# Moving some VectorE products of an S4-convolution and MLP kernel to GpSimd, with a new written-out order

## The chip, the cores and the metric

One core of a Trainium2 chip runs the kernel. A core has five engines with a queue each, called here as the profile calls them: PE (TensorE, matmuls), ACT (ScalarE), DVE (VectorE), POOL (GpSimd) and SP (SyncE, which issues most DMAs). A queue is worked off in order; between queues there are semaphores. The metric is the device time of one execution in microseconds, lower is better. Three runs of the kernel before took 517.82, 519.9 and 520.2 us, median 519.9.

## The reference

The input is `u` of 2048 tokens by 512 channels, in float32. With `xn = layernorm(u)` the output is `u + s * silu(b)`.

`s` is a long convolution per channel (S4): from complex parameters A, B and C of 512 channels by 128 states and a step `dt = exp(log_dt)` a kernel of 2048 taps is made,

```python
logdA = dt * A                       # 512 x 128, complex
P = exp(logdA[:, :, None] * l)       # l = 0 .. 2047
K = einsum("dn,dnl,dn->dl", C, P, dt * B).real
s = irfft(rfft(pad(xn)) * rfft(pad(K)))[:2048] + xn * Dskip
```

`b` is a mixer: `h = gelu(layernorm(xn) @ w1)`, whose four channel groups are shifted by +1, −1, +2 and −2 tokens, then `x1 = xn + shifted(h) @ w2`, then `b = x1 + gelu(layernorm(x1) @ w3) @ w4` with 1376 hidden channels.

## The kernel before, in words

The kernel is written as a plan. Python code calls `V`, `A`, `T`, `Q` (DVE, ACT, PE, SP) and `E` (either ACT or DVE) in the order of the mathematics; each call becomes an operation of the plan with a number, the engines that may do it (`alts`), a cost and the operations it depends on. Nothing is issued then. At the end `Plan.issue` walks through `ORDER`, a text of 1583 numbers, and issues the operations in that order. So every engine's queue is its part of that text. A mark behind a number chooses the engine where there is a choice: a for ACT, v for DVE, no mark for the first of `alts`. The profile therefore puts every operation on one line, L309, and tells them apart by the names of their tiles.

The work falls into these parts:

- Parameters (`params`, operations 36 to 77). Some thirty small steps on tiles of 128 x 512 make, for every channel and state, the logarithm of the decay (`pn[:, 0]`), the phase per step, the start phase and the amplitude. They need A, B, C and `log_dt`; scratch is the tile `tm`. PE transposes the four results, and four copies of 128 x 512 bring them into `par`.
- Token mixing (`token_mixing`): layer norm of X, transposes, `w1` (three of eight pairs of token groups in float32, five in split float16), gelu to `hT`, then `w2` with the shifts. On the way X's first transform is made (`u_stage1`, tile `ue`, stored to `scr_Ud`). The weights w3 and w4 are read once for a scale (`weight_squares`, tile `wst`) and once to be split (`prep`).
- Tables (`tables`): the kernel K in 16 chunks of 32 channels, in four blocks of four. A block makes exponentials per row (`EB`, `mag`, on ACT) and phases (`pab`). A chunk then makes phases in 32-bit integers in a tile `wv` (three DVE instructions), takes cosine and sine on ACT (three instructions of 128 x 2080), and multiplies by magnitudes on DVE (`factors` and `sums`): `eg` from two parts of `EB`, `wv` by `eg` (128 x 2048), the lower half from `mag` and the upper (128 x 2048), `up` from two parts of `mag`, and two products of `wv` by `up`. Then 256 records of matmul on `wv` give the taps (`pc<-wv`), and a first transform (`kev`, `k1e`) goes to memory.
- MLP (`mlp`, eight groups of 256 tokens): per step 24 matmuls by w3 (`pb`), gelu (`g32`), a split of the result in two float16 halves (`ghl`, one scaling on ACT or DVE, one difference on DVE), and 12 matmuls by w4 (`pa`).
- Products (`products`, 16): spectra of X and K by matmuls, a complex product on DVE (`pr`, `kh`), the inverse (`z1e`) to memory. Eight of them are interleaved with chunks 8 to 15 and the MLP, eight come after.
- End: `inverse` and `finish`: the last transform, times silu, plus the input, stored.

Tiles lie at addresses written out by hand. The ring `egr` has two places, used in turn by `eg` and `up` (and `rem` of a block); so an `eg` can be written when the last one has been read, and the same for `up`. The waves' tiles (`wv`) take turns in two buffers, `phA` and `phB`; `pn` and `tm` of the parameters lie in `phA`, the float32 w1 in `phB`. The matmul `warm` on the identity (operation 2, 40 matmuls) fills PE at the start; operation 1 is a square root on ACT of no further use.

Of the kernel before, what the change touches and what calls it, by code (L numbers as in the profile page):

```python
# [14 lines left out]
ALU = mybir.AluOpType  # L15
# [4 lines left out]
P = 128  # L20
# [6 lines left out]
MAGIC = 12582912.0  # L27
# [11 lines left out]
CQ = 32  # L39
# [71 lines left out]
3 17 78 0 16 42 20 19 36 38 4 31 14 39 44 40 70 15 41 21 43 45 22 8 103 105 1 7 46 106 104 107 5 71a 503 6 47 108 13 2  # L111
109 110 88 111 504 112 89 505 24 48 50 90 114a 79 91 80 506 81 92 113a 115a 93 23 51 94 82 95 83 49 118a 84 85 52 96a
100a 86 87a 508 101 97a 98 509 102a 99a 166 162 160 119 164 167 163 116 9 121 165 120a 117a 18 161 37 168 169 72 10
143 144 170 171 53 172 26 73a 25 54 122 123 511 173 55 124 174 125 175v 178v 140 126 127 177v 11 199v 179a 141 196v
128 215 200 59 146 145 149a 213 32 147a 28 142 27 129 219 56 188 339 180 176v 197 217 60 182v 183 218 270 266 184a 158
130 150 268 131 216 269 185 271 181a 186 191 267 272 214 220 273 132 221 30 274 133 340 148 34 61 189 222 275 152 223
276 277 57 64 224 225 134 62 187 29 192a 193 194a 195 226 58 76 227 345 136v 63 230v 65 231v 516 66 68 190 208 67 202
203 513 211a 212 209v 210 198 229v 69 137 201 138v 74 77a 341 514 515 244 247a 248 235v 75v 245a 228v 507 205 206 207
232v 512 246 510 261 236 237 278 233 234 517 346 249v 139 241 242 135 204 279 518 519 238 239 522 262a 12 263 264a 297
252v 343 243 280 155 240 265 255 256 156 536 537 520 282v 521 253 250 151 251 288v 298v 258 254 300a 538 525 259 299  # L120
# [12 lines left out]
390 641 642 628 669 721a 727 722 708 709 723 485a 717 738 733 745 654 739 670 746 486 671 643a 653 656 675 728a 734a
735 724 729 730 672 731 644 673 674 740 657 658 747 645 752 753 741a 646a 676 787 742 820 660 788 736 659 759a 647a
789 760a 754 795 648 678 767 768 748a 791 774 677 797 661 662 663a 790 737 798 743 744 438 440 460 749 750 751 755a
775 761 762 763a 792 793 664 799 680 665 666a 756 667a 461 796 458 679 757 794 681 682 758 769 800 781 764a 801 765
776 770a 683a 777a 802 854 684 685 771 803 772 782 453 451 773 834 835 766 1092 1093 1085 1086 778 806 779 804 668 809
836 805 807 459 1094 686a 687a 1087 783a 454 808 780 688 784 837 838 1099 1100 785 1095a 822 810 811 843 1088a 840
1096 812 813 1089 1114 1106a 868 814a 815 1107a 1115 786 839 816 817a 818a 1090 1091 819 1108 1116 869 841 870 842 441
823 1109 1097 1101 1102a 1103 824a 825 826 1110a 856 1111v 827 1098 828 829 1121 871 845 1104 1105 872 873 830 844  # L140
831a 1128 439 1112 1117a 1113 1118 832a 452 846 487 847 848a 874 1122 902 849 903 488 1129 904 1119 1123 850 1134
1130a 1131 1124a 1125 833 855 851a 852a 905 875 857 908 890 858a 876 1135 1136 1120 859 1126 1127 877 860 906 853 1148
878 888 1149 1141 907 861 944 862 863 864 866a 865a 1142 1143 867 889 879 911 880 881 909 1150 1132 936 910 1163 937
1144v 1170 938 1137a 1138 882a 883 939 941 942 884 489 1133 940 1145 946 1164 1171 885a 886a 891 913 947 943 949 950
892a 1139 893 948 1140 922 1151a 894 490 895 1152 1146 1147 887 1153 1155a 1156a 924 896 897 1159a 1157 898 1154 1158
912 951 1160a 1165 899a 914 1166a 915 900a 1161 945 1177 1167 983 984 985 952 1168 916a 917 1169 1172 1162 1183 1173v
958 1174 953 918 1175 954 1176 919a 920a 955 956 989 1178 925 1184 901 923 1179a 926a 927 957 1185 1186a 1190 928 1191
1180 1187 986 1204a 929 1181 930 921 931 1192 1197 932 988 933a 960 959 987 969 971 1182 934a 1198 992 961 935 962
1188 990 963a 1189 970 1199 964 1017 1018 1193a 965 1200a 966a 967a 968 1201 1219 1194 1208a 972 1005 1195 1209a 1019
973a 991 1205a 1212 1213 1206 974 994 1210 1211 975 976 1196 1207 1202 1003 1020 1214 1203 1022 977 978 979 1021 980a  # L150
981a 982 1023 1220 1221 993 1026 995 1222a 1024 1004 996 1232 997a 998 1051 999 1000a 1052 1226 1001a 1006 1215a 1025
1039 1053 1233 1227 1007a 1216 1008 1239 1240 1054 1055 1217 1009 1010 1011 1012 1013 1014a 1015a 1028 1027 1060 1223
1056 1234 1218 1029 1030 1031v 1037 1032 1224 1241 1228v 1033 1002 1034a 1057 1058 1016 1038 1246 1229 1035a 1040 1261
1041a 1042 1059 1036 1043 1044 1539 1071 1484 1045 1046 1253a 1247 1225 1230 1248 1062 1047 1073 1538 1049a 1048a 1050
1061 471 1231 1536 473 1268 472 474 1063 491 1064 492 1269 1065a 1066 1067 1371 1072 1262 1242a 1235v 1068a 1069a 1385
1236 1074 1237 1254v 1075a 1070 1255 1263 1243 1256 1076 1372 1077 1238 1257v 493 1078 1244 1245 1373 1249a 1250 1387
# [1128 lines left out]
```

## Time and profile before

| | |
|---|---|
| Runs | 517.82, 519.9, 520.2 us |
| The profiled execution | 516.23 us, span from first to last instruction 514.4 us |
| Granted TensorE clock | 0.996 |
| Busy: PE, DVE, ACT, POOL | 489.2, 452.4, 404.4, 0.7 us |
| ACT table loads | 57, 73.1 us together |
| Memory traffic | 90.07 MB, 175 GB/s on the mean |

A row of the timeline has its start in us from the span's start, the time it took, the engine, the operation, the tile written and the tiles read, shapes, and in brackets how long the engine stood still before it and what ended that. A row of the groups has the count, the busy time and mean length of one in ns, and the idle time before. A row of a stage has the busy time of PE, PEld (weight loads), DVE, ACT and POOL, with the number of instructions in brackets, then the granted clock, the DMA engines' busy share and GB/s. A matmul in float32 appears as two records. A busy PE is not always PE at its peak, since the ends of matmuls are modelled.

### The profile page before, as it was taken

The numbers are of one execution on the slowest core, as the hardware profiler recorded it, in microseconds if no ns is written. First come the engines' busy times: TensorE is split into PE (matmuls) and PEld (weight loads), VectorE is DVE, ScalarE is ACT, GpSimd is POOL, SyncE is SP. The second block draws the span as 40 slices with busy tenths as digits, with TensorE's granted clock in tenths as the row PEclk, the third lists the DMA queues.
The fourth block names the chain that finished last, engine by engine and source line by source line (L and its number), as shares of the span: only waits on it lengthen the run. The fifth ranks groups of instructions, "written<-read, shape, count | busy, mean of one in ns | idle before, by whom it ended". The sixth has DMA issues, their size and how long they took to land.

```text
span 514.4 us, 14347 instructions
## 1 busy us (share of the span) xinstructions
PE 489.2 (95%) x6209; PEld 313.8 (61%) x6209; DVE 452.4 (88%) x634; ACT 404.4 (79%) x596; POOL 0.7 (0%) x6
## 2 busy tenths in 40 slices
PE   3899899999999999999999989999999999999993
PEld 3766566664555867667566645657565565576451
DVE  5999999999999999999999989999985578756466
ACT  3999999979998599999999999997865356256320
POOL 0000000000000000000000000000000000000000
PEclk9999999999999999999999999999999999999998
DMA  8957999757362650443635646185689998887987
GB/s 227 250 143 246 274 264 267 203 183 164 42 154 59 150 103 2 66 80 42 145 76 133 145 100 149 64 177 164 137 213 249 243 301 253 245 272 226 331 255 206
DMA packets 149393, 90.07 MB, mean 175 GB/s; under 512 B 97681, under 2 KB 135825, under 8 KB 148945
## 3 DMA queue, kind: packets, MB, share of 16 engines
q1 hardware_dynamic: 144800, 84.68, 65.0%
q10 hardware_dynamic: 4528, 4.46, 3.0%
q8 instruction: 49, 0.80, 0.7%
q14 instruction: 16, 0.12, 0.1%
HBM read 52.95 MB, written 29.36 MB: 160 GB/s over the span
## 4 chain that ended last, share of the span: by engine, by line
PE 65%; DVE 16%; ACT 10%; DMA 4%; issue 3%; ACTq 0%; SPq 0%; DVEq 0%
PE pb L309 25%; PE pa L309 22%; PE pc L309 13%; DVE wv L309 5%; PE pd L309 5%; DVE X L309 2%; ACT ue L309 2%; ACT L309 2%; DMA scr_Ud<-ue 2%; ACT mag L309 1%; DMA X<-in_A_u_dram 1%; ACT wv L309 1%; DVE pr L309 1%; DMA x1T<-x1h 1%; DVE eg L309 1%
## 5 line engine op out<-in xcount | busy, mean ns | idle before, releaser
L309 PE MATMUL pb<-x1T,w3h 128*128 128x256 f16 (+1 forms) x1056 | 124.8, 273 | 0.1
L309 PE MATMUL pa<-w4h,ghl 128*128 128x512 f16 (+1 forms) x528 | 122.1, 380 | 0.0
L309 PEld LDWEIGHTS <-w3h 128*128 128x128 f16 (+1 forms) x1056 | 102.0, 100 | 26.3 <-issue 10.7
L309 PEld LDWEIGHTS <-ghl 128*128 128x128 f16 (+1 forms) x528 | 49.1, 98 | 62.4 <-issue 10.2
L309 ACT ACT_TABLE_LOAD x57 | 73.1, 1283 | 4.8 <-issue 3.1
L309 ACT ACTIVATE wv<-wv 128x2080 f32<-128x2080 int32 x32 | 62.9, 1964 | 1.1 <-DVE wv L309 0.9
L309 ACT ACTIVATE g<-pb,wsc 128x512 f32<-128x512 f32 (+1 forms) x48 | 30.6, 649 | 11.5 <-PE pb L309 11.3
L309 DVE TENSOR_TENSOR wv<-wv,eg 128x2048 f32<-128x2048 f32 x16 | 36.6, 2286 | 2.2 <-ACT wv L309 2.0
L309 DVE SCALAR_TENSOR_TENSOR ghl<-g,wsc,ghl 128x512 f16<-128x512 f32 (+1 forms) x48 | 33.2, 701 | 5.9 <-ACT ghl L309 5.8
L309 DVE TENSOR_TENSOR wv<-mag,wv 128x2048 f32<-128x2048 f32 x16 | 36.5, 2284 | 0.0
L309 DVE TENSOR_TENSOR pr<-pd,kh 128x1024 f32<-128x1024 f32 x16 | 19.6, 1224 | 18.5 <-ACT kh L309 13.7
L309 PEld LDWEIGHTS pc<-wv 128*32 128x32 f32 x2048 | 29.9, 109 | 7.9 <-issue 5.1
L309 PE MATMUL pc<-wv 128*32 128x64 f32 x2048 | 32.8, 220 | 1.7 <-issue 1.7
L309 ACT ACTIVATE mag<-par 128x128 f32<-128x128 f32 x132 | 32.9, 462 | 0.0
L309 ACT ACTIVATE wv<-wv,halfpi 128x2080 f32<-128x2080 f32 x16 | 32.8, 2051 | 0.1
L309 ACT ACTIVATE ghl<-g,wsc 128x512 f16<-128x512 f32 (+1 forms) x38 | 25.4, 678 | 6.6 <-PE pa L309 4.5
L309 PE MATMUL pb<-xT,w1h 128*128 128x256 f16 x240 | 27.8, 273 | 0.4 <-DMA xT<-x2h 0.3
L309 PEld LDWEIGHTS <-w1h 128*128 128x128 f16 x240 | 23.1, 98 | 7.5 <-issue 5.0
L309 PE MATMUL pb<-w,hT 128*128 128x512 f32 x58 | 26.8, 599 | 0.0
L309 PE MATMUL pa<-w,hT 128*128 128x512 f32 x58 | 26.5, 598 | 0.0
L309 PE MATMUL pb<-xT,w 128*128 128x256 f32 x96 | 22.6, 384 | 0.7 <-ACT hT L309 0.7
L309 DVE TENSOR_TENSOR wv<-par,ev 128x1056 int32<-128x1056 f32 x16 | 20.1, 1254 | 1.5 <-PE pc L309 1.5
(156 smaller groups left out, 810.6 us busy)
## 6 DMA issues: line engine op xcount, KB each, us to landing
wst<-in_B_w_dram SPq DMA_DIRECT2D x20, 512.0 KB, 4.6
scr_Ud<-ue SPq DMA_DIRECT2D x16, 512.0 KB, 4.7
uin<-scr_Ud SPq DMA_DIRECT2D x16, 512.0 KB, 4.7
scr_Kfa<-k1e SPq DMA_DIRECT2D x8, 512.0 KB, 5.4
cst<-c_gp SPq DMA_DIRECT2D x16, 256.0 KB, 4.8
kin<-scr_Kfa SPq DMA_DIRECT2D x8, 512.0 KB, 4.7
scr_Kfb<-k1e SPq DMA_DIRECT2D x8, 512.0 KB, 5.8
scr_Zda<-z1e SPq DMA_DIRECT2D x8, 512.0 KB, 3.2
```

The lines of the kernel that those rows point to most:

```text
L309: ins = [getattr(self.engines[op.eng], name)(*args, **kw).ins for name, args, kw in op.calls]
```

## The change

A helper `Spare` is added, called `G` in the kernel: its operations may run on DVE or on POOL, and the plan counts POOL at twice DVE's cost. `G` takes the place of `V` in `factors` (the product `eg`), in `sums` (the product `up`) and in 22 steps of `params`. For such an operation the mark a now means POOL. The two halves of w1 in float32 move from `phB` to the places of blocks 8 and 9 of the ring for `hT`. The copies into `par` write in the order of memory (`n p r`) instead of in strides. The constants in the plan stay. The text `ORDER` is another one throughout: the order on each engine, the engine where there is a choice, and the order of DMA issues on SP and ACT.

```diff
 class Plan:
     def __init__(self, nc):
-        self.engines = {"PE": nc.tensor, "ACT": nc.scalar, "DVE": nc.vector, "SP": nc.sync}
+        self.engines = {
+            "PE": nc.tensor, "ACT": nc.scalar, "DVE": nc.vector, "SP": nc.sync, "POOL": nc.gpsimd,
+        }
...
-            op.eng = {"a": "ACT", "v": "DVE"}.get(word[-1]) or list(op.alts)[0]
+            op.eng = {"a": list(op.alts)[-1] if "POOL" in op.alts else "ACT", "v": "DVE"}.get(word[-1]) or list(op.alts)[0]
...
+class Spare:
...
+    def __getattr__(self, name):
+        def call(*args, **kw):
+            cost = dve_cost(name, args)
+            call = (name, args, kw)
+            self.plan.add(
+                {"DVE": (cost, call), "POOL": (2 * cost, call)}, args[:1], [a for a in args[1:] if is_ap(a)]
+            )
+
+        return call
...
-        load_w(w1, w1s, Ring(phB, K4, 2), Q)
+        load_w(w1, w1s, Ring(sblocks + 8 * K4, K4, 2), Q)
...
-        V.tensor_mul(pn[:, 0], raw["Ar"], dtb)
+        G.tensor_mul(pn[:, 0], raw["Ar"], dtb)
...
-        V.tensor_mul(ta, raw["Bi"], raw["Cr"])
-        V.tensor_add(wi, wi, ta)
+        G.tensor_mul(ta, raw["Bi"], raw["Cr"])
+        G.tensor_add(wi, wi, ta)
...
-            E.copy(par[:, k].rearrange("n (p r) -> n r p", r=4), pt.rearrange("n (r p) -> n r p", r=4))
+            E.copy(par[:, k].rearrange("n (p r) -> n p r", r=4), pt.rearrange("n (r p) -> n p r", r=4))
...
-        outer(V.tensor_mul, eg, EB[:, sl, R_EGA : R_EGA + 4], EB[:, sl, R_EGB : R_EGB + 8])
+        outer(G.tensor_mul, eg, EB[:, sl, R_EGA : R_EGA + 4], EB[:, sl, R_EGB : R_EGB + 8])
...
-        V.tensor_mul(up, mag[:, :, low], mag[:, :, 32:33].to_broadcast([P, CQ, 32]))
+        G.tensor_mul(up, mag[:, :, low], mag[:, :, 32:33].to_broadcast([P, CQ, 32]))
```

The two orders begin like this (the first line of each; parameter steps on POOL such as 44a and 45a follow in the second):

```diff
-3 17 78 0 16 42 20 19 36 38 4 31 14 39 44 40 70 15 41 21 43 45 22 8 103 105 1 7 46 106 104 107 5 71a 503 6 47 108 13 2
+0 16 17 3 4 20 36 78 18 15 37v 7 42v 14 41v 8 43v 88 89 72 90 5 6 79 91 80 44a 73a 511 81 82 83 92 19 38 84 85 93 94
```

More of the change, by code (lines that the diff above doesn't have):

```diff
@@ L116 @@
[L116 to L120, printed above, removed]
@@ new lines @@
+228v 182v 341 343 57a 64a 272 504 133 157 148 505 270 190 175a 179v 268 149a 150 342 183 180 184v 269 347 181a 266
+232v 345 267 271 344 506 177v 61a 273 62a 63a 65a 66a 274 349 275 67a 187 191 276 155 156 277 202 192v 231v 68a 205
+206 194a 278 195 208 196v 513 279 280 197 233 199v 200 229v 136v 193 198 201 203 350 355 235v 236 211v 209v 212 244
+514 515 210 138v 348 353 58a 76 137 69 74 204 247a 245a 237 139 135 346 248 31 230v 234 207 508 75v 507 509 525a 282v
+510 517 238 252v 518 77a 246 239 288v 261 253 249v 241 242 250 354 351 240 255 256 264a 262v 297 265 356 361 281v 512
@@ new lines @@
+327 564 404 393 383 384 405 567 552 581 580 535 553a 566 411 568 406 569 336 333 334 582a 585a 407 394 604 408 388 329
+418 419a 403 385 395a 583 596 597 598 425 570a 599 601 602 330 151 571 584 554a 605 420 555 421 424 426 412 572 606
+396 442 607 608 443a 429 600 603 413 573a 586 609 414 427 587 428 445 415 448 435 416 430 574a 422a 610 611 332 417
+618a 409 410 401 446a 444 465 615a 449 450 431 423 462 612 613 335 588 589 629 436 432 433 434 495a 499a 437 590a 630
+468 500v 631 466a 467 501 496a 497 575 591 463a 464 614 632 634 455 633 447 616 635a 469 481 592 593a 502 710a 470 456
@@ new lines @@
+769 752 749 753 754 796 664 665 737 743 744 750 751 666a 791 763a 667a 800 790 770a 781 440 439 792 441 451 452 793
+794 801 774 775 668 680 681 682 802 803 755v 756 757 854 776 764v 758 765 782 453 458 771 809a 772 683v 684 685 834
+805 835 836 777a 778 806a 804 807 686a 687a 837 839 808 838 766 840a 1092 773 783v 1093 810 779 780 811 459 1085 473
+1086 843a 812 813 784 821 785 1087 841 874a 814a 815 816 1099 868 1106a 1088a 1089 786 1094 688 869 870 817a 842 822
+818a 823 845 856 824a 1100 1101 825 826 827 1090 1091 871 1095a 873 872 828 1121 1114 819 1115 829 830 831a 844 877a
@@ new lines @@
+1102v 1103 1096 1122 832v 1110a 833 1107v 1108 1109 846 847 848a 1111v 1112 849 454 487 1097 875 876 1116 474 850 1098
+1117a 488 489 851a 852a 1123 1104 1105 1124a 857 858a 902 903 904 905 855 1128 1129 1113 878 859 1118 908a 1134 1135
+853 907 1141 1142 906 860 861 862 863 864 922 879 911a 1119 866a 1136 1125 888 865v 880 881 1120 1126 1143 882a 909
+910 883 884 867 1127 946 890 936 885a 937 940 886a 490 1130v 1131 1132 913 941 471 912 1155a 1137a 1144a 1145 891 938
+939 892a 1133 889 947 1163 1164 942 893 1148 948 958a 1149 1138 894 895 1156a 896 897 1157 1139 1140 887 944 943 949
@@ new lines @@
+1159a 898 899v 1165 950 951 1146 914 915 945 900a 916a 969 917 1147 1150 1151v 918 1170 1177 1152 1160v 919v 920v 983
+984 1153 1154 1161 1171 952 954 953 955a 1158 1172 924 925 926a 1178 1166v 1167 1173a 985 1168 1169 956 957 901 923
+927 928 929 930 1162 1183 1190 1184 986 988 931 960 959 932 987 933a 1179v 1180 1191 934a 971 961 1192 962 963a 1185
+1174 989a 990 1175 1176 1204a 1017 935 1197 964 1181 965 1198 921 966a 1018 1019 991 970 1186v 1187 967a 968 972 1193v
+1194 1208v 1020 1182 1212 1199 1213 973a 974 1188 992a 1189 1195 1022 994 1021 1003 975 976 1200a 977 472 978 979 981a
@@ new lines @@
+1201 1023a 993 1219 980a 982 1209a 1210 1024 1057a 1005 995 996 1196 997a 998 1202 1205a 999 1206 1051 1214 1215a
+1000a 1001a 1052 1037 1053 1220 1006 1007a 1226 1227 1004 1025 1207 1221 1008 1054 1026a 1203 1216 1217 1218 1056 1039
+1211 1009 1010 1011 1012 1013 1232 1028 1027 1014a 1029 1060a 1030 1002 1015a 1055 1016 1038 1239 1031v 1032 1228v
+1537 1033 1240 1034a 1035a 1229 1040 1036 1058 1222v 1041a 1233 1223 1234 1073 1042 1059 1043 1224 1225 1241 1230 1044
+1045 1046 1047 1049a 1061 1261 1048a 1050 1071 1062 1063 1064 1413 1400 491 492 1065v 1066 1262 1246 493 1371 1072
@@ new lines @@
+1486 1067 1247 1068a 1069a 1235v 1236 1253v 1254a 1231 1488 1070 1074 1538 1237 1372 1238 1075a 1242v 1243 1244 1373
+1255 1076 1256 1248 1249a 1250 1245 1268 1257a 1258a 1251 1077 1079 1386 1078 1080 1387 1259 1081 1083v 1260 1263
+1264a 1082a 1385 494 1275 1374 1376 1252 1375a 1536 1265 1266 1399 1377 1378 1401 1379 1276 1269 1380 1381 1383v 1270
+1271v 1272 1382a 1084 1415 1281 1539 1388 1389a 1390 1267 1277a 1391 1428 1282 1392 1273 1384 1393 1394 1483 1395 1283
+1397a 1493 1441 1274 1278 1396v 1402 1403a 1398 1414 1404 1405 1427 1406 1288 1289 1290 1279 1407 1408 1409 1455 1484
@@ new lines @@
+1310 1410v 1284v 1416 1429 1443 1411a 1418 1295 1296 1285 1280 1286 1442 1302a 1303v 1417a 1419 1420 1421 1422 1457
+1291a 1423 1424v 1311 1304 1305 1430 1425v 1432 1287 1292 1431a 1293 1433 1434 1294 1435 1436 1437 1439v 1412 1471
+1297 1456 1298a 1317 1299 1438a 1306a 1307a 1444 1445a 1446 1440 1308 1447 1300 1318 1448 1312 1324 1496 1449 1450
+1309 1451 1313v 1301 1314 1452a 1458 1507 1453v 1460 1325 1337 1315 1494 1338 1319 1470 1320a 1321 1426 1454 1469
+1459a 1461 1462 1463 1464 1465 1467v 1540 1330 1466a 1472 1473a 1492 1499 1474 1475 1476 1541 1477 1495 1543 1316 1331
@@ new lines @@
+1332 1322 1326a 1542 1468 1478 1479 1344 1481a 1480v 1482 1500 1497 1518 1510 1501 1345 1485 1562 1498 1502 1339 1556
+1323 1327 1333a 1328 1340a 1346 1329 1490 1351 1352 1565 1334 1335 1336 1347v 1503 1508 1521 1353 1511 1527 1489 1512
+1487 1509 1505 1365 1348 1513 1544 1358 1359 1516 1571 1506 1522 1519 1341 1547 1553 1530 1523 1342 1343 1354v 1349
+1350 1515 1355 1366 1360 1361a 1362 1356 1357 1367v 1504 1517 1368 1363 1364 1369 1520 1524 1525 1528 1577 1370 1491
+1531 1529 1545 1532 1548 1514 1546 1554 1533 1549 1526 1555 1534 1550 1535 1557 1563 1558 1566 1551 1564 1552 1559
@@ L172 @@
+1560 1567 1572 1568 1573 1561 1569 1570 1574 1576 1575 1 1578 1579 1580 1582 1581
 """
@@ L385, in __getattr__, with __init__ @@
         return call
+class Spare:
+    def __init__(self, plan):
+        self.plan = plan
+    def __getattr__(self, name):
[6 more added lines that the diff above has]
+        return call
 class Either:
@@ L633, in params @@
         pn = phtile([P, 4, 4, NM], "pn")
-        V.tensor_mul(pn[:, 0], raw["Ar"], dtb)
+        G.tensor_mul(pn[:, 0], raw["Ar"], dtb)
         V.scalar_tensor_tensor(pn[:, 1], raw["Ai"], INV_2PI, dtb, op0=ALU.mult, op1=ALU.mult)
-        V.tensor_scalar(raw["Ai"], pn[:, 1], MAGIC, -MAGIC, op0=ALU.add, op1=ALU.add)
-        V.tensor_sub(pn[:, 1], pn[:, 1], raw["Ai"])
+        G.tensor_scalar(raw["Ai"], pn[:, 1], MAGIC, -MAGIC, op0=ALU.add, op1=ALU.add)
+        G.tensor_sub(pn[:, 1], pn[:, 1], raw["Ai"])
         tm = phtile([P, 4, 4, NM], "tm")
         wr, wi, ta, tb = tm[:, 0], tm[:, 1], tm[:, 2], tm[:, 3]
-        V.tensor_mul(wr, raw["Br"], raw["Cr"])
-        V.tensor_mul(ta, raw["Bi"], raw["Ci"])
-        V.tensor_sub(wr, wr, ta)
-        V.tensor_mul(wi, raw["Br"], raw["Ci"])
-        V.tensor_mul(ta, raw["Bi"], raw["Cr"])
-        V.tensor_add(wi, wi, ta)
+        G.tensor_mul(wr, raw["Br"], raw["Cr"])
+        G.tensor_mul(ta, raw["Bi"], raw["Ci"])
+        G.tensor_sub(wr, wr, ta)
+        G.tensor_mul(wi, raw["Br"], raw["Ci"])
+        G.tensor_mul(ta, raw["Bi"], raw["Cr"])
+        G.tensor_add(wi, wi, ta)
         A.activation(ta, wr, AF.Abs)
@@ L654, in params @@
         V.reciprocal(ta, ta)
-        V.tensor_mul(rat, rat, ta)
-        V.tensor_mul(ta, rat, rat)
+        G.tensor_mul(rat, rat, ta)
+        G.tensor_mul(ta, rat, rat)
         A.activation(tb, ta, AF.Sqrt, bias=1.0)
-        V.tensor_mul(am, am, tb)
-        V.tensor_mul(am, am, dtb)
+        G.tensor_mul(am, am, tb)
+        G.tensor_mul(am, am, dtb)
         A.activation(ph, rat, AF.Arctan)
-        V.tensor_scalar(ph, ph, INV_2PI * CYCLE, None, op0=ALU.mult)
-        V.tensor_scalar(ta, ph, -2.0, 0.25 * CYCLE, op0=ALU.mult, op1=ALU.add)
-        V.tensor_mul(ta, ta, swap)
-        V.tensor_add(ph, ph, ta)
-        V.tensor_scalar(tb, wr, 0.0, None, op0=ALU.is_lt)
-        V.tensor_scalar(ta, ph, -2.0, 0.5 * CYCLE, op0=ALU.mult, op1=ALU.add)
-        V.tensor_mul(ta, ta, tb)
-        V.tensor_add(ph, ph, ta)
-        V.tensor_scalar(tb, wi, 0.0, -2.0, op0=ALU.is_lt, op1=ALU.mult)
+        G.tensor_scalar(ph, ph, INV_2PI * CYCLE, None, op0=ALU.mult)
+        G.tensor_scalar(ta, ph, -2.0, 0.25 * CYCLE, op0=ALU.mult, op1=ALU.add)
+        G.tensor_mul(ta, ta, swap)
+        G.tensor_add(ph, ph, ta)
+        G.tensor_scalar(tb, wr, 0.0, None, op0=ALU.is_lt)
+        G.tensor_scalar(ta, ph, -2.0, 0.5 * CYCLE, op0=ALU.mult, op1=ALU.add)
+        G.tensor_mul(ta, ta, tb)
+        G.tensor_add(ph, ph, ta)
+        G.tensor_scalar(tb, wi, 0.0, -2.0, op0=ALU.is_lt, op1=ALU.mult)
         V.scalar_tensor_tensor(ph, tb, 1.0, ph, op0=ALU.add, op1=ALU.mult)
```

70 lines of the change are left out of this document (15 added, 55 removed).

## The prediction

> **What bounds the kernel now.** I read the page first: span, busy time by engine, slices.
>
> ```profile
> span 514.4 us, 14347 instructions
> PE 489.2 (95%) x6209; PEld 313.8 (61%) x6209; DVE 452.4 (88%) x634; ACT 404.4 (79%) x596; POOL 0.7 (0%) x6
> DVE  5999999999999999999999989999985578756466
> ```
>
> PE looks like the bound, but DVE fills every slice of the first three quarters too. So I cut the span where DVE's nines end, at the last table chunk, with busy time by stage (PE, weight loads, DVE, ACT, POOL in that order).
>
> ```profile
> 0.00:60.00 60.00, 47.73 (x257) 36.85 (x259) 54.11 (x144) 50.72 (x102) 0.70 (x6) 1.00 0.84 219
> 60.00:120.00 60.00, 58.94 (x591) 38.73 (x588) 57.56 (x89) 54.64 (x64) 0.00 (x0) 1.00 0.88 230
> 120.00:240.00 120.00, 120.00 (x1420) 75.67 (x1419) 118.35 (x144) 112.18 (x189) 0.00 (x0) 1.00 0.43 87
> 240.00:380.20 140.20, 138.29 (x2313) 88.55 (x2310) 136.75 (x145) 129.64 (x174) 0.00 (x0) 1.00 0.57 130
> 380.20:514.40 134.20, 124.21 (x1637) 73.96 (x1634) 85.65 (x117) 57.27 (x70) 0.00 (x0) 0.99 0.88 256
> ```
>
> Up to 380.2 us DVE works 54.11 + 57.56 + 118.35 + 136.75 = 366.8 us and stands still for 13.4; PE is idle for 380.2 − 365.0 = 15.2, most of it in the first 60. After 380.2 DVE is busy for 64% only. Who waits for whom shows in the timeline, at the last chunk's products:
>
> ```profile
> 378.99 1.22 DVE L309 TENSOR_TENSOR wv<-up,wv 128x1024 f32<-128x1024 f32 x1
> 380.35 1.60 PE L309 MATMUL pc<-wv 128*32 128x64 f32 x97
> ```
>
> DVE's last product of chunk 15 ends at 380.21 and PE's matmuls on it begin at 380.35. Chunk 9 looks the same:
>
> ```profile
> 260.89 1.22 DVE L309 TENSOR_TENSOR wv<-up,wv 128x1024 f32<-128x1024 f32 x1
> 262.25 2.01 PE L309 MATMUL pc<-wv 128*32 128x64 f32 x128
> ```
>
> The gap is 0.14 us in both. PE has other matmuls to fill the waits, which is why it counts as busy, but the tables reach it as fast as DVE makes them. Up to 380 us DVE's queue sets the pace, with ACT and PE close behind.
>
> **The change, part by part.** What leaves DVE: the marks in the new order put all 32 `eg` and `up` products and 18 of the 22 rewritten parameter steps on POOL (12 products, sums and differences; 6 with one tensor); steps 37, 41, 42 and 43 carry no a, so stay on DVE.
>
> ```profile
> L309 DVE TENSOR_TENSOR up<-mag 128x1024 f32<-128x1024 f32 x16 | 19.6, 1222 | 0.3
> L309 DVE TENSOR_TENSOR eg<-EB 128x1024 f32<-128x1024 f32 x16 | 19.5, 1220 | 0.2
> L309 DVE TENSOR_TENSOR tm<-rawC 128x512 f32<-128x512 f32 x4 | 2.7, 686 | 3.9 <-DMA rawC<-in_A_B_im_dram 3.2 <-DMA rawC<-in_A_C_re_dram 0.7
> L309 DVE TENSOR_SCALAR tm<-pn 128x512 f32<-128x512 f32 x3 | 1.3, 421 | 0.0
> ```
>
> That is 19.6 + 19.5 + 12 × 0.69 + 6 × 0.42 = 49.9 us. What comes to DVE: the new order also gives DVE steps that ACT did. Ahead of chunk 15's last product I count by the marks 11 more `ghl` scalings, 4 `ue` copies, 3 `z1e`, 2 `kev`, 2 `k1e`, 1 `xT` (PSUM copies of 128x512), 6 `x1h` casts, 8 more scalings of the `x2h`, `x`, `x1n`, `w3h` and X kind, and 2 pairs of statistics steps.
>
> ```profile
> L309 DVE TENSOR_SCALAR ghl<-g,wsc 128x512 f16<-128x512 f32 (+1 forms) x10 | 4.7, 470 | 4.4 <-ACT g L309 2.9 <-PE pa L309 1.5
> L309 DVE COPY ue<-pa 128x1024 f32<-128x1024 f32 x2 | 2.4, 1220 | 0.9 <-DMA scr_Ud<-ue 0.9
> L309 DVE COPY z1e<-pc 128x512 f32<-128x512 f32 x5 | 3.4, 690 | 3.4 <-PE pd L309 3.4
> L309 DVE CAST x1h<-x1n 128x512 f16<-128x512 f32 x3 | 1.3, 424 | 0.1
> L309 DVE BATCH_NORM_STATS2 stats<-X 128x6 f32<-128x512 f32 x32 | 20.9, 679 | 0.4 <-DMA X<-in_A_u_dram 0.4
> ```
>
> 11 × 0.47 + 4 × 1.22 + 8 × 0.69 + 6 × 0.42 + 8 × 0.5 (between the `ghl` and `z1e` rows) + 2 × 0.85 = 23.8 us. Net, DVE has 26.1 us less to do before the point that sets the pace. Also, three groups of twelve `w3h` matmuls have moved behind chunk 15 in PE's order. The chain of waits has such a group at 1.31 us:
>
> ```profile
> 225.37 1.31 PE pb L309 x12
> ```
>
> So 3 × 1.31 = 3.9 us of PE work is left for later. The span changes by −26.1 + 3.9 = −22.2 us, plus whatever DVE loses because POOL now works beside it. That loss is the whole question. POOL does no arithmetic beside DVE in this trace; the nearest rows are its start-up.
>
> ```profile
> 0.24 0.10 POOL L1273 MEMSET const-float32-0.0<- 128x1 f32 x1 [0.24 <-issue]
> ...
> 0.73 0.20 POOL masks.py:197 MEMSET ident<- 128x128 f32 x1 [0.29 <-POOLq L1273]
> ...
> 0.81 0.06 DVE L309 MEMSET epst<- 128x1 f32 x1 [0.81 <-PEq L1273]
> ...
> 1.01 0.29 POOL masks.py:199 TENSOR_SCALAR_AFFINE_SELECT ident<-ident 128x128 f32<-128x128 f32 x1
> ```
>
> ```profile
> L309 DVE MEMSET hw<- 128x1 f32 x6 | 0.4, 59 | 0.0
> ```
>
> POOL's length first: 0.29 us for 128 elements; with 0.10 of it fixed (the 128x1 memset) 1024 elements take 1.65, in proportion 2.3. I take 2.0 for a table product and 1.0 for a parameter step: 32 × 2.0 + 18 × 1.0 = 82 us (69 to 96). DVE's loss: at least zero, since nothing POOL does can shorten a DVE instruction. At most all the time that POOL works, less what DVE then spends on PSUM or statistics. Eleven groups of that kind, from the `stats` rows above (20.9) and `pr` below (19.6) down to the `ue` copies (2.4), sum to 100 of DVE's 452 us, 22%.
>
> ```profile
> L309 DVE TENSOR_TENSOR pr<-pd,kh 128x1024 f32<-128x1024 f32 x16 | 19.6, 1224 | 18.5 <-ACT kh L309 13.7 <-PE pd L309 4.8
> L309 DVE TENSOR_SCALAR wv<-wv 128x2080 int32<-128x2080 int32 x16 | 19.8, 1239 | 0.0
> L309 DVE TENSOR_TENSOR wv<-wv,eg 128x2048 f32<-128x2048 f32 x16 | 36.6, 2286 | 2.2 <-ACT wv L309 2.0
> ```
>
> The other 78% draws two elements of SBUF per step: `wv<-wv` gets through 1.68 elements per ns of one tensor, `wv<-wv,eg` 0.90 of two tensors each. POOL's products are two-tensor reads of SBUF as well. So the upper end is 0.78 × 82 = 64 us. The DVE memset of 0.06 us beside POOL's memset is as long as the later ones alone (59 ns), but neither reads anything; the rows that the new load is nearest to are the two-tensor products, so I stand nearer the upper end: 45 us, 70% of it. The rest is hidden because a POOL product has a chunk's time (262.25 to 380.35 for six chunks, 20 us) for 4 us of work, and can slip to where DVE reads PSUM or stands idle.
>
> The Trainium skill states this as a rule: by "SBUF — State Buffer", section "Who interferes with whom", a VectorE instruction with two SBUF inputs, or one in a two-port mode, and a GpSimd instruction that reads SBUF take one shared read port in turn, and the later one blocks for the whole of the other. By that rule the upper end would hold; the unstretched memset agrees with its exception for instructions that only write. By the 4.5 us that "GPSIMD Engine Reference", section 3.1, gives for 2048 elements a table product would be 2.2 us, an estimate, and the upper end 69.
>
> The new waits: DVE's first product of a chunk (`wv<-wv,eg`) now waits for POOL, and behind it in DVE's queue stand the `ghl` differences that PE's `pa` matmuls need. At 4 us of POOL work per 20 us I cost it at nothing; if POOL could run only in DVE's gaps it would be late, and DVE would then wait instead of being slowed: the same loss.
>
> The start:
>
> ```profile
> 7.79 1.09 PE L309 MATMUL pc<-ident,pn 128*128 128x128 f32 x4 [7.79 <-DVE pn L309]
> 8.68 10.87 PE L309 MATMUL pa<-ident 128*128 128x128 f32 x80
> 8.92 1.10 ACT L309 COPY par<-pc 128x512 f32<-128x512 f32 x1 [2.57 <-PE pc L309]
> 8.93 0.51 ACTq L309 DMA_DIRECT2D X<-in_A_u_dram  x1
> ...
> 19.38 0.60 PE L309 MATMUL pd<-ident,x 128*128 128x128 f32 x4
> ...
> 20.66 1.13 PE L309 MATMUL pd<-ident,x 128*128 128x128 f32 x8 [0.68 <-ACT x L309]
> ...
> 24.02 3.62 PE L309 MATMUL pb<-xT,w 128*128 128x256 f32 x16
> ```
>
> ACT's second load of X was issued at 8.93, behind a copy that waited for PE; now it stands ahead of that copy. The first parameter transpose needs one product instead of three, so the warm-up matmuls (10.87) end about 1.5 us sooner, and the first real matmul at 24.02 stands behind two transposes instead of five; the last three took from 20.66 to 24.02, so 3.4 us sooner. While DVE sets the pace this only lets PE wait longer. w1 away from the waves' buffer, the contiguous `par` copies (four) and the moved square-root warm-up are worth under 1 us each, hidden behind DVE's queue. On SP's queue three weight-square loads now stand ahead of the first `scr_Ud` stores; PE waited for `ue` once, for 1.6 us, and I cost that at nothing, at most one such wait more.
>
> ```profile
> PE pa L309 <- ACT ue L309: 1.6, 1, 1.6
> ```
>
> Sum: 514.4 − 22.2 + 45 = 537.2 us, 22.8 us longer. The profiled execution took 516.23 us, 1.8 around its span; the median of the runs is 519.9, 3.7 above it. I add the difference to the median, 519.9 + 22.8: **543 us**.
>
> **The rivals.** *No loss (faster).* If POOL and DVE do not touch each other, DVE is 26.1 us ahead and PE becomes the bound. PE's idle time before 380.2 is 15.2 us, of which some 6.5 before its first instruction stay; I take back the 3.4 at the start and 2.6 of the rest. That is −6: 514 us. For it: DVE is full and POOL empty, and the memset. Against it: nothing in the trace shows the two reading together. It decides below a loss of 19.6 us. *Full hold.* All 64 us are lost: −22.2 + 64 = +42, 562 us. *A draw*: a loss of 19.6 to 24.8 us uses up the relief, 517.3 to 522.5. *POOL late at the start*: eleven parameter steps in a row on POOL, 11 us against some 6 on DVE, before chunk 0; 5 us that the earlier start covers, and no sign of its own. *The change not doing what it says*: only the four unmarked parameter steps, under 3 us.
>
> **How the numbers follow.** What a measurement of this kernel can tell from no change is about 0.5%, 2.6 us. My forecast (loss 25 to 55) has 0.37, the full hold 0.20, no loss 0.33, the draw 0.10. Slower is 0.57, same 0.10, faster 0.33. The likeliest case alone spans 523 to 553. Both signs hold much of the chance, so the range must take in the no-loss case down to 511 and part of the full hold up to 560.
>
> **What would show it.** Right: `wv<-wv,eg` (2286 ns), `wv<-mag,wv` and the shift of `wv` (1239) longer on the mean, with maxima stretched by up to a POOL product; PSUM readers such as `pr<-pd` unchanged at 1224; DVE still full until past 390 us; PE waiting for `wv` and `ghl`. Wrong: DVE's means unchanged, idle time appearing in DVE before 370 us, and PE's `pc<-wv` of chunk 15 starting before 375. A POOL product far from 2.0 us moves the sum by 32 times the difference, times the lost share.

## The result and the profile after

The changed kernel took 554.33 us in the median of four runs (553.01 to 554.86), the kernel before 519.65 us in four runs beside it (517.82 to 520.2). The ratio is 1.0661, with a 95% interval of 1.064 to 1.0682: slower by 6.6%, where the prediction named 543 us. The profiled execution took 553.01 us. Its page, span and busy time first, then DVE's row of slices:

```profile
span 551.1 us, 14366 instructions
PE 496.2 (90%) x6209; PEld 313.2 (57%) x6209; DVE 478.4 (87%) x621; ACT 380.4 (69%) x558; POOL 114.2 (21%) x56
DVE  4999899999999999999999989998985758756366
```

DVE gave 50 steps away and is nevertheless 26 us longer busy than before (478.4 against 452.4). The last nine of its row stands in the same slice as before, but a slice is 13.8 us long now instead of 12.9. The stages, cut where chunk 15's last product ends, and that place in the timeline:

```profile
0.00:60.00 60.00, 46.00 (x237) 35.37 (x239) 48.55 (x122) 44.29 (x98) 24.92 (x24) 0.94 0.85 216
60.00:120.00 60.00, 52.21 (x586) 35.98 (x585) 59.19 (x81) 51.51 (x57) 16.46 (x6) 1.00 0.85 225
120.00:240.00 120.00, 111.10 (x1172) 65.09 (x1171) 118.89 (x142) 97.35 (x166) 30.87 (x11) 1.00 0.36 74
240.00:414.55 174.55, 159.47 (x2549) 99.41 (x2547) 166.91 (x167) 127.23 (x167) 41.93 (x16) 0.99 0.51 113
414.55:551.10 136.55, 127.44 (x1672) 77.32 (x1670) 84.84 (x112) 60.05 (x74) 0.00 (x0) 0.98 0.90 255
```

```profile
413.32 1.22 DVE L311 SCALAR_TENSOR_TENSOR wv<-up,wv 128x1024 f32<-128x1024 f32 x1
...
414.67 2.02 PE L311 MATMUL pc<-wv 128*32 128x64 f32 x128
```

The last product now ends at 414.54 instead of 380.21, and PE's matmuls follow 0.13 us later, as before. So 34.3 of the span's 36.7 us are there already; the rest takes 136.6 us instead of 134.2. From 60 us on DVE is busy 344.99 of 354.55 us, while PE and ACT stand still for 31.8 and 78.5. DVE is the bound, alone now.

Next the lengths of single instructions: tile views of the waves, the spectra and the two POOL products (count, then minimum, median and maximum in ns).

```profile
L311 DVE TENSOR_SCALAR wv<-wv x16: 1229/1243/2873, 70.9 to 388.7; 128x2080 int32<-128x2080 int32 x16
L311 DVE TENSOR_TENSOR wv<-wv,eg x16: 2258/2282/3387, 83.8 to 402.6; 128x2048 f32<-128x2048 f32 x16
L311 DVE TENSOR_TENSOR wv<-mag,wv x16: 2278/2286/3981, 86.5 to 405.9; 128x2048 f32<-128x2048 f32 x16
```

```profile
L311 DVE TENSOR_TENSOR pr<-pd,kh x16: 1216/1224/1225, 278.1 to 495.3; 128x1024 f32<-128x1024 f32 x16
...
L311 DVE TENSOR_TENSOR pr<-kh x16: 691/692/2266, 281.2 to 498.4; 128x512 f32<-128x512 f32 x16
```

```profile
L311 POOL TENSOR_TENSOR eg<-EB x16: 1947/3787/4329, 76.7 to 382.0; 128x1024 f32<-128x1024 f32 x16
```

Before, the last of the three waves' rows had its maximum within 0.01 us of its median:

```profile
L309 DVE TENSOR_TENSOR wv<-mag,wv x16: 2262/2284/2290, 76.4 to 371.1; 128x2048 f32<-128x2048 f32 x16
```

The medians are the old lengths, the maxima lie 1.1 to 1.7 us above them. `pr<-pd,kh`, which reads PSUM, never moves from 1.22; its neighbour `pr<-kh`, which reads SBUF alone, does. An `eg` on POOL takes 1.95 us when it is undisturbed, but its median is 3.79. The timeline at 106 us shows why:

```profile
106.11 2.29 DVE L311 TENSOR_TENSOR wv<-mag,wv 128x2048 f32<-128x2048 f32 x1
106.27 3.93 POOL L311 TENSOR_TENSOR eg<-EB 128x1024 f32<-128x1024 f32 x1 [9.33 <-DVE wv L311]
108.43 2.85 DVE L311 SCALAR_TENSOR_TENSOR wv<-up,wv 128x1024 f32<-128x1024 f32 x1
111.21 1.21 DVE L311 TENSOR_TENSOR wv<-up,wv 128x1024 f32<-128x1024 f32 x1
```

`eg` starts 0.16 us after DVE's product; its record is 1.98 us too long, about the time that DVE's product still had to run. Then DVE's next product, 1.22 us long elsewhere, takes 2.85: it begins at 108.43 and gets through only after `eg` has ended at 110.20. They took turns, very nearly a whole instruction at a time. I compared every DVE instruction with the usual length of the same operation, tiles and shape before. 44 are longer by over 0.06 us, 46.7 us together, and every one of them overlaps a POOL instruction.

### The profile page after: what moved, and what is told of

It is laid out like the page before. It is cut to its first block, busy times and chain, and to the rows that moved or that the text cites. A ratio compares the mean times of both kernels' runs of the same rounds, so it can differ in the third digit from the quotient of the medians.

```text
span 551.1 us, 14366 instructions
## 1 busy us (share of the span) xinstructions
PE 496.2 (90%) x6209; PEld 313.2 (57%) x6209; DVE 478.4 (87%) x621; ACT 380.4 (69%) x558; POOL 114.2 (21%) x56
## 4 chain that ended last, share of the span: by engine, by line
DVE 57%; PE 28%; issue 8%; ACT 4%; DMA 1%; SPq 0%; ACTq 0%; DVEq 0%
DVE wv L311 26%; PE pa L311 9%; PE pb L311 9%; PE pc L311 6%; DVE X L311 5%; DVE ghl L311 5%; PE pd L311 4%; DVE stats L311 3%; DVE pr L311 2%; DVE pab L311 2%; DVE x1h L311 2%; DVE w3h L311 1%; DVE kh L311 1%; DVE w4h L311 1%; DVE ue L311 1%
## 5 line engine op out<-in xcount | busy, mean ns | idle before, releaser
L311 POOL TENSOR_TENSOR eg<-EB 128x1024 f32<-128x1024 f32 x16 | 52.3, 3269 | 117.2 <-DVE wv L311 100.1
L311 POOL TENSOR_TENSOR up<-mag 128x1024 f32<-128x1024 f32 x16 | 37.1, 2318 | 149.7 <-DVE wv L311 72.3
L311 DVE SCALAR_TENSOR_TENSOR ghl<-g,wsc,ghl 128x512 f16<-128x512 f32 (+1 forms) x48 | 37.8, 790 | 9.6 <-ACT ghl L311 8.9
L311 DVE TENSOR_TENSOR wv<-mag,wv 128x2048 f32<-128x2048 f32 x16 | 39.1, 2443 | 0.0
L311 PE MATMUL pc<-kev,kk 32*128 32x256 f32 x128 | 18.6, 409 | 10.0 <-DVE kev L311 10.0
```

What stands on the lines that cost most here:

```text
L311: ins = [getattr(self.engines[op.eng], name)(*args, **kw).ins for name, args, kw in op.calls]
```

## The experiments

All ratios are against the kernel before on the same chip. "Chunk 15" is the time at which DVE ends its last product; "records" is the sum of the recorded lengths of DVE's instructions up to there. Neighbouring records overlap a little (1.22 us of record, 1.13 from start to start), so the busy time is less than that sum, and the overlap is a term of its own.

**All 50 steps back on VectorE, new order.** `44a` becomes `44` in the order text, and so on for the 50.

> The changed kernel with its order, but all 50 moved steps (32 table products, 18 parameter steps) back on VectorE; GpSimd does nothing. Theory (exclusion: a GpSimd product and a two-tensor or fast one-tensor VectorE instruction never run side by side, so the move gives back what it takes): VectorE gets 49.9 us of work and loses the 46.7 us by which its instructions were stretched, so it reaches the last product of chunk 15 within 8 us of the 414.5 us of the changed kernel, and the time is 545 to 560 us; no VectorE instruction is longer than in the kernel before. Rival A (GpSimd is the whole cost, the order is as good as the old one): the time falls back to 517 to 526 us. Rival B (the moved steps gain something although instructions are stretched): over 565 us.

555.98 us (554.12 to 556.71), ratio 1.0708 (1.068 to 1.0737). Its stages up to chunk 15:

```profile
0.00:60.00 60.00, 44.14 (x239) 34.89 (x241) 50.77 (x141) 44.31 (x98) 0.70 (x6) 0.98 0.85 221
60.00:417.80 357.80, 328.00 (x4304) 204.35 (x4300) 343.04 (x420) 276.20 (x388) 0.00 (x0) 0.97 0.51 117
```

DVE is busy 393.8 us up to chunk 15 at 417.8, against 393.5 up to 414.5 with POOL at work. No DVE instruction is stretched; the waves' rows have their old means again:

```profile
L311 DVE TENSOR_TENSOR wv<-mag,wv 128x2048 f32<-128x2048 f32 x16 | 36.6, 2286 | 0.0
L311 DVE TENSOR_TENSOR wv<-wv,eg 128x2048 f32<-128x2048 f32 x16 | 36.6, 2284 | 0.5
```

So with this order it hardly matters where the 50 steps run: the move gives back what it takes, as the theory says, and rival A falls. What makes the kernel slow is there without POOL.

**One half of the move each.** Marks taken off the 18 parameter steps, or off the 32 table products.

> The changed kernel with the 18 parameter steps back on VectorE, the 32 table products on GpSimd. Theory (each part of the move is a draw by itself): VectorE gets some 11 us of steps back and loses about as much stretch in the first 50 us, the time is 548 to 559 us. Rival (the parameter steps on GpSimd make the start late: chunk 0's last product came at 91.1 us instead of 81.4): it comes at 81 to 85 us and the time is under 547 us.

> The changed kernel with the 32 table products back on VectorE, the 18 parameter steps on GpSimd. Theory (a draw by itself): VectorE gets 39.1 us of products and loses the some 35 us of stretch that lies behind 60 us, the time is 550 to 561 us. Rival A (the table products on GpSimd lose more than they take off): under 547 us. Rival B (they gain): over 564 us.

553.5 us (ratio 1.0664, 1.0635 to 1.0693) and 554.35 us (1.0663, 1.062 to 1.0706). Each half is a draw by itself. Chunk 0's last product comes at 90.9 us without the parameter steps on POOL, 91.1 with them, 81.4 before: the late start isn't theirs.

**GpSimd that only writes.** The product is replaced by two memsets, with the same waits, here for `eg` and likewise for `up`:

```diff
-        outer(G.tensor_mul, eg, EB[:, sl, R_EGA : R_EGA + 4], EB[:, sl, R_EGB : R_EGB + 8])
+        with plan.together():
+            G.fill(eg, EB[:, sl, R_EGA : R_EGA + 4], EB[:, sl, R_EGB : R_EGB + 8])
```

> The changed kernel with each of the 32 table products replaced by two memsets of the same tile to 0.5 on GpSimd: GpSimd is about as busy and everybody waits as before, but it reads no SBUF. Left out: the products eg and up (the taps K come out as other numbers). Theory (the lock is on reading): the two-tensor rows of wv keep their old lengths (2286, 1222 ns), the last product of chunk 15 comes 25 to 45 us sooner than 414.5, the time is 515 to 532 us. Rival A (any GpSimd work beside VectorE, or its semaphores, slows VectorE): the same stretches as with products, 545 us or more. Rival B (fast one-tensor steps are held by writes too): the shift of wv (1240 ns) is stretched and the two-tensor products are not, 530 to 545 us.

521.98 us (one run), chunk 15 at 382.8. The tile views:

```profile
L311 DVE TENSOR_SCALAR wv<-wv x16: 1223/1243/1999, 71.3 to 356.2; 128x2080 int32<-128x2080 int32 x16
L311 DVE TENSOR_TENSOR wv<-wv,eg x16: 2257/2282/2293, 82.7 to 370.8; 128x2048 f32<-128x2048 f32 x16
L311 DVE TENSOR_TENSOR wv<-mag,wv x16: 2273/2285/2287, 85.3 to 374.2; 128x2048 f32<-128x2048 f32 x16
```

```profile
L311 POOL MEMSET eg<- x32: 945/952/2042, 69.1 to 354.2; 128x1024 f32 x32
```

POOL is about as busy (two memsets of 0.95 us), but from 60 us on not one two-tensor product is stretched, and of the 34.7 us by which the changed kernel was slower 32.4 are gone. (Before 60 us the parameter products still run on POOL and stretch DVE by 10 us.) Only the fast one-tensor steps are still held at times (`wv<-wv`, up to 2.0 instead of 1.24). The price of the move is the reading, not the semaphores, the lateness or the order of POOL's work. This does not contradict the run with everything back on VectorE: the move takes some 50 us off DVE and the stretches give nearly all of them back, and without the stretches the relief is large enough to hide the steps that came from ACT.

**GpSimd that reads one tensor.** The product is replaced by a copy.

> The changed kernel with each of the 32 table products replaced by a copy on GpSimd that reads one tensor of SBUF instead of two, same output size. Left out: the second factor of eg and up (the taps K come out as other numbers). Theory (one reader at a time, whatever it reads): a VectorE instruction that meets a copy is stretched by nearly the copy's whole length, as with products; by so much as a copy is shorter than a product (1.9 us) the time falls below 554, and no further: 540 to 556 us if a copy takes 1.5 to 1.9 us. Rival (the two share the reading, so one stream costs half of two): stretches of half a copy or less, and the time near the 522 us of the kernel that only writes, under 538 us.

531.69 us (one run). The time falls under the rival's bound, but for another reason: a copy takes 1.04 us and not 1.5 to 1.9.

```profile
L311 POOL COPY eg<-EB x16: 1042/2895/3438, 67.9 to 361.0; 128x1024 f32<-128x1024 f32 x16
```

The longest stretch of a DVE instruction by a copy is 0.84 us, four fifths of a copy where the rival had half at most, and a copy's median of 2.9 us is a copy and a long DVE product. My bounds mixed up the two theories, since I had the length wrong; the stretches speak for turns of whole instructions.

**The pairs by themselves.**

> No mixer is computed; it copies some of the input to the output, and in 16 stages runs eight VectorE instructions of one kind beside ten GpSimd instructions of one kind, started together. Kinds on VectorE: two (product of two SBUF tensors 128x1024), one (scaling of one SBUF tensor 128x1024), pin (product of a PSUM and an SBUF tensor 128x512), sta (batch-norm statistics 128x512). Kinds on GpSimd: none, mul (two tensors, 128x1024), copy (one tensor), fill (memset). Theory (one at a time, whole instructions): two takes 1.22 us alone, 3.0 to 3.2 on the mean beside mul (its own length and a product's 1.9), 2.2 to 2.4 beside copy, 1.22 beside fill; one is held by mul, copy and fill; pin and sta keep their lengths beside all. Rival (a shared rate, slower but side by side): two beside mul 1.6 to 2.4 us, beside copy less than 1.8, and pin is stretched too, since it also reads SBUF.

VectorE's instructions were put in another order than the program's text, so a name such as `two_none` doesn't tell what ran beside it; the times do. The timeline:

```profile
8.67 32.87 POOL L44 TENSOR_TENSOR g<-a,b 128x1024 f32<-128x1024 f32 x10 [2.20 <-DMA b<-in_A_u_dram]
...
22.87 3.35 DVE L37 TENSOR_TENSOR two_mul<-x,y 128x1024 f32<-128x1024 f32 x1
26.15 3.35 DVE L37 TENSOR_TENSOR two_none<-x,y 128x1024 f32<-128x1024 f32 x1
...
44.82 1.21 DVE L37 TENSOR_TENSOR two_mul<-x,y 128x1024 f32<-128x1024 f32 x1
...
46.16 18.85 POOL L45 COPY g<-a 128x1024 f32<-128x1024 f32 x10 [4.62 <-DVE g L62]
...
49.13 2.05 DVE L37 TENSOR_TENSOR two_copy<-x,y 128x1024 f32<-128x1024 f32 x1
...
65.26 10.88 POOL L46 MEMSET g<- 128x1024 f32 x10 [0.25 <-DVE g L62]
66.25 1.22 DVE L37 TENSOR_TENSOR two_copy<-x,y 128x1024 f32<-128x1024 f32 x1
...
75.17 1.51 DVE L38 TENSOR_SCALAR one_none<-x 128x1024 f32<-128x1024 f32 x1
...
77.26 0.68 DVE L38 TENSOR_SCALAR one_none<-x 128x1024 f32<-128x1024 f32 x1
...
81.27 2.82 DVE L38 TENSOR_SCALAR one_mul<-x 128x1024 f32<-128x1024 f32 x1
...
109.80 14.70 POOL L45 COPY g<-a 128x1024 f32<-128x1024 f32 x10 [4.29 <-DVE g L62]
...
110.86 0.68 DVE L38 TENSOR_SCALAR one_copy<-x 128x1024 f32<-128x1024 f32 x1
...
135.77 19.28 POOL L44 TENSOR_TENSOR g<-a,b 128x1024 f32<-128x1024 f32 x8 [0.99 <-DVE g L62]
...
137.93 0.67 DVE L39 TENSOR_TENSOR pin_copy<-z,x 128x512 f32<-128x512 f32 x1
138.52 0.68 DVE L40 BATCH_NORM_STATS2 sta_mul<-x 128x6 f32<-128x512 f32 x1
```

A two-tensor product takes 1.21 us alone, 3.35 beside POOL's products, 2.05 beside its copies and 1.22 beside its memsets. A fast scaling takes 0.68 alone, 2.82 beside products and 1.51 beside memsets. Products with a PSUM operand and statistics stay at 0.67 and 0.68 with POOL's products at work from 135.77 on. In the first stretch one DVE and one POOL product alternate with a period of 3.28 us. Alone they take 1.13 and 2.41 us from start to start (19.28 / 8 for POOL), 3.54 together, so they run one behind the other but for about 0.26 us.

That is the theory in the main, and the rival, a shared rate, falls, above all by `pin`, which reads SBUF too. Two things came otherwise. The sizes (3.0 to 3.2 and 2.2 to 2.4 us were expected) missed, because a product of full tensors takes 2.34 us on POOL and not 1.9, and because the 0.26 us were not reckoned with. And the fast scalings were not held by copies as expected: back to back they kept their 0.68 us, one of 0.92 apart, and the first copy waited instead, with a record of 4.44 us. So the two engines need not alternate one for one.

**The old order: small parts, move, split.** Four kernels on the old order separate what the new text mixes: the two small parts alone; with them the 32 products on POOL (`522` to `522a` and so on); the new split between ACT and DVE (69 marks changed); and both.

> The kernel before, its order and its split, with only the two small parts of the change: w1 in its new place and the contiguous parameter copies. GpSimd does nothing. Theory: both are hidden, 517 to 521 us, no difference that can be measured. Rival (they cost something, and the run with only the table products on GpSimd owed part of its 14 us to them): 523 us or more.

> The old order and the old split between ScalarE and VectorE, with only the 32 table products marked for GpSimd (parameters on VectorE; w1's place and the contiguous parameter copies as in the change). Theory (exclusion): VectorE loses 39.1 us of work and gets 32 stretches of up to 1.6 us, 35 to 51 us, so the time is 516 to 532 us, about the old time, and the rows of wv have maxima 1.5 us over their medians. Rival A (no loss): 508 to 515 us, no stretched row. Rival B (GpSimd's products come late and VectorE waits for them): over 535 us, with VectorE idle for eg or up.

> The kernel before with its order, GpSimd unused, but each of the 69 steps that changed sides between ScalarE and VectorE is on the side that the changed kernel gives it (plus the two small parts). Theory (the steps given to VectorE are most of the slowdown): VectorE gets the 27.0 us by which it is busier up to chunk 15 in the changed kernel with everything on VectorE (393.8 against 366.8), and reaches that point at 402 to 412 us; the time is 538 to 555 us. Rival (the new order's waits are the loss, the steps find room): under 530 us.

> As the run with only the new split in the old order, and the 32 table products on GpSimd as well. Theory (a draw wherever VectorE is the only bound): within 8 us of the run with only the new split. Rival (the move costs 14 us in the old order whatever the split): 10 to 20 us over it.

| order, split | products on VectorE | products on GpSimd |
|---|---|---|
| old, old | 518.26 us, 0.9982 (0.9958 to 1.0006) | 533.04 us, 1.0275 (1.025 to 1.0299) |
| old, new | 548.06 us, 1.0537 (1.05 to 1.0573) | 561.1 us, 1.0793 (1.0772 to 1.0814) |
| new, new | 555.98 us, 1.0708 (1.068 to 1.0737) | 554.33 us, 1.0661 (1.064 to 1.0682) |

In the last row the 18 parameter steps move as well. The small parts cost nothing. The split alone costs 30 us in the old order, nearly the whole loss: it gives DVE 22.6 us of records ahead of chunk 15, and moves that point from 383.4 to 408.0. Both came as the theory had it. In the old order the products on POOL cost 13 to 15 us under either split, so there my draw failed. With the new split the rival (10 to 20 us) held; with the old one 533.04 us lies between the theory (up to 532) and its Rival B (over 535, waits for `eg` or `up`), and neither held. Stages of the old order from 60 us to chunk 15: the new split, then the old split with the products on DVE, then the old split with them on POOL:

```profile
60.00:408.00 348.00, 328.98 (x4340) 207.15 (x4339) 333.76 (x416) 282.40 (x396) 0.00 (x0) 0.99 0.55 124
```

```profile
60.00:383.40 323.40, 320.03 (x4324) 204.03 (x4324) 314.25 (x378) 298.65 (x428) 0.00 (x0) 0.99 0.58 133
```

```profile
60.00:396.10 336.10, 319.79 (x4324) 203.28 (x4324) 304.16 (x349) 298.26 (x428) 85.18 (x31) 1.00 0.57 128
```

With the move DVE does less (304.2 against 314.3; only 25.1 us of stretch against 39.1 us of products), and yet chunk 15 comes 12.7 us later than with them on DVE: DVE's idle time up to there rises from 17.1 to 40.1 us. Those waits:

```profile
DVE wv L311 <- ACT wv L311: 7.0, 7, 1.6
DVE pr L311 <- PE pd L311: 4.5, 4, 1.7
DVE wv L311 <- PE pc L311: 3.9, 4, 1.4
```

Most are for ACT and PE, few for POOL (1.8 us for `eg`, 1.6 for `up`). The old order is laid out for instructions of known length, and what is stretched here leaves a neighbour waiting there. Which stretch causes which wait I have not traced.

**The old order with GpSimd that only writes.** The move as it would be if nothing were shared.

> The kernel before with its order and split, each of the 32 table products replaced by two memsets on GpSimd of the same tile. Left out: the products eg and up (the taps K come out as other numbers). It prices the move if nothing had to be shared. Theory A (the prediction's rival without loss: VectorE free, TensorE the bound): 505 to 514 us. Theory B (queues written out by hand leave nothing to gain: whoever is freed waits for the next): 515 to 521 us.

519.14 us (one run) beside 519.89 us of the kernel before. The stage:

```profile
60.00:382.90 322.90, 318.46 (x4324) 203.70 (x4324) 280.54 (x346) 298.31 (x427) 58.95 (x60) 1.00 0.58 133
```

DVE has 34 us less to do and stands still for 50.7 us up to chunk 15, which comes at 382.9, where it was (383.4). PE is busy 318.5 of 322.9 us. Theory B holds: in this order DVE's freed time does not shorten the kernel.

**The old split in the new order.** The 69 marks of the old split, everything else as changed.

> The changed kernel, GpSimd's 50 steps kept, but each of the 69 steps that changed sides between ScalarE and VectorE goes back to the engine that it had in the kernel before (same place in the order). Ahead of chunk 15's last product VectorE loses 39 steps, some 24 us by the prediction's count, and gets 3 back. Theory (the move to GpSimd is a draw, the steps given to VectorE in exchange are the loss): the last product of chunk 15 comes at 388 to 396 us instead of 414.5, the time is 525 to 537 us. Rival (the order or GpSimd's lateness holds it): it stays over 545 us.

599.17 us, ratio 1.1543 (1.1511 to 1.1575): the theory missed by far. The rival's bound (over 545) held, but not its reason: the time did not stay where it was, it rose by 45 us. DVE's waits:

```profile
DVE ghl L311 <- ACT ghl L311: 25.9, 9, 9.7
DVE x1h L311 <- ACT x1h L311: 11.3, 4, 7.8
DVE x2h L311 <- ACT x2h L311: 7.2, 1, 7.2
```

The steps did leave DVE (458.3 us busy instead of 478.4), but stand in ACT's queue at places chosen for DVE's, and DVE waits 44 us for those three alone. This undoes no part of the change; it makes a new mismatch. The split had to be put into the old order to be priced.

None of these versions beats the kernel before; the nearest is the one with the small parts alone, whose interval holds 1.

## Why the prediction was right or wrong

The direction and the mechanism were right, and 543 us was 11 too low. The range from 511 to 560 us held both signs, so that 554 lies in it says little; the terms say more. By the prediction's own terms, in us of records up to chunk 15 (the column of the runs from the changed kernel, the one with all steps back on DVE, and the kernel before):

| | predicted | measured |
|---|---|---|
| 50 steps off DVE | −49.9 | −49.8 (all steps back: 39.0 + 10.8) |
| steps from ACT | +23.8 | +23.4 (428.1 − 404.7) |
| stretched by POOL | +45 | +46.2 (424.5 − 428.1 + 49.8) |
| less overlap of neighbouring records | not in the sum | +7.0 (37.9 to 30.9) |
| DVE idle | 0 | +7.6 (13.4 to 21.0) |
| chunk 15's last product | +18.9 | +34.3 |
| what follows it | +3.9 | +2.4 |
| span | +22.8 | +36.7 |

The medians differ by 34.7 us and not by 36.7, since the profiled execution lay 3.4 us under the median before and 1.3 under it after.

- The three terms of the prediction are within 1.2 us. Two were counted from rows. The third, 45, was picked between 0 and 64 ("70% of it") and no row gave it, so that it came so near is partly luck. POOL's time is 32 products at 1.9 us (predicted 2.0) and 24.3 us for the parameters, whose records hold some waiting: 86 in all, against 82. The lost share is 0.54 of that, against 0.55. The rule of the Trainium skill, "SBUF — State Buffer", section "Who interferes with whom", that one waits for the whole of the other, and that a GpSimd instruction which only writes does not hold a two-input one, agrees with 3.35 us beside products and 1.22 beside memsets. That it also counts the fast one-tensor modes agrees with 0.68 against 2.82. "The whole" is in these runs all but some 0.26 us.
- The failed step is "The span changes by −26.1 + 3.9 = −22.2 us, plus whatever DVE loses", a sum of record lengths that left out overlap and waits. A record is some 0.07 us longer than the time it takes from the queue: the 50 steps that left were worth 3.4 us less than their records (34.3 us of overlap with them, 30.9 without), and the new order overlaps 3.6 us less before that. Of the idle time, 5.6 us lie in the first 60 us (DVE 48.55 busy instead of 54.11).
- "5 us that the earlier start covers": the first real matmul did come 3.4 us sooner (20.66 instead of 24.02), but chunk 0's last product came 9.7 us later. It is as late with POOL idle (90.5) and with only the new split in the old order (90.2, against 83.8 with the small parts alone), so most of it comes with the steps given to DVE at the start, and not with the parameter steps on POOL.
- The rival without loss had its mechanism right and its price wrong. Without a lock the new order takes 521.98 us and the old one 519.14, not 514. The prediction read "DVE's queue sets the pace" and took back 6 us of PE's idle time; but PE is busy 318.5 of 322.9 us from 60 us on with DVE freed, and the relief was worth nothing, while 22.6 us more on DVE cost 30. That bound is one-sided.
- The full hold is wrong as a sum, not in its mechanism: where the two meet, the hold is nearly full (2.85 us instead of 1.22, so 1.63 of `eg`'s 1.95), but over the kernel it took 0.54 of POOL's time, not 0.78.
- "A draw" did not come as the prediction had it, at the old time, but as a draw between two slow kernels: 555.98 and 554.33 us.
- Signs: medians kept and maxima up by a POOL product, `pr<-pd,kh` unchanged, DVE full past 390 us were right. PE waits less for `wv` (3.2 us) and `ghl` (2.2) than for `kev` (10.0) and `ue` (5.8), the DVE steps that the new order queues behind the products.

Left open: why the new order without POOL is 8 us slower than the old one with the same split, how much of any loss is the lower clock below, and by which waits the move costs 13 us and more in the old order when it is a draw in the new one.

## What to carry to other kernels

Before work is moved to GpSimd beside a busy VectorE, look at what stands in VectorE's queue: beside two-tensor reads of SBUF or fast one-tensor steps the two took turns here, nearly a whole instruction at a time, and the move was a swap at best. Where two engines were full at once, 22.6 us more on VectorE cost 30 us and 34 us less on it gave nothing, so don't hand over other work in exchange for a relief that hasn't been measured. An order and a split that were made for each other couldn't be undone by halves (599 us): price each in the order where it fits.

## What was not expected of the hardware

PE's granted clock, 1.00 in the kernel before until 510 us, halves in the changed kernel's start:

```profile
40.00:45.00 5.00, 1.55 (x8) 0.94 (x8) 5.00 (x12) 0.29 (x1) 4.51 (x4) 0.90 0.93 295
45.00:50.00 5.00, 4.65 (x10) 2.02 (x11) 4.90 (x19) 4.19 (x7) 0.00 (x0) 0.50 0.16 39
50.00:55.00 5.00, 5.00 (x23) 4.29 (x21) 4.51 (x8) 4.97 (x17) 0.00 (x0) 0.92 0.85 233
```

PE worked 1.55 of 5 us; it waited for scalings of x on DVE, some of which POOL's parameter steps stretched. From 44.0 us on the clock was 0.50 for 6.8 us. POOL's steps are not needed for this: with them back on DVE and the table products on POOL a drop of the same length comes near 58 us. The lower clock lasts 3.4, 6.8 or 10.2 us in these traces, and 0 us in all in the kernel before, 10.2 in the changed one, 20.5 with all steps back on DVE and 51.2 with the old split in the new order (up to the last drop at the end). The Trainium skill, "TensorE: Matmul & The Clock Gate", section "Part 1: The HAM clock gate", tells of windows of 3413 ns, after an idle one of which the clock halves; these lengths agree, being one, two and three windows. But PE was not idle ahead of the drop: it worked 0.78 us of the 3.4 before it (40.6 to 44.0). Work that is late on another engine may so slow the matmuls behind it as well; no run here prices that by itself.

The records of POOL hold its waits for its turn: `eg` has 1.95 us of its own and 3.79 in the median, so the busy time of POOL in these profiles is more than its work. And the length hangs on the operands: 1.90 to 1.95 us for the kernel's products of broadcast operands, 2.34 to 2.41 for products of full tensors of the same output size, 1.04 for a copy, 0.95 for a memset.
